# Two pairs of copies left unordered, and one band of input loaded earlier, in a dilated neighborhood attention kernel

## The chip, the cores and the metric

The kernel runs on one core of a Trainium2 chip. Its time is the device time in microseconds of that core, from one launch. The kernel before takes 312.07 us (median of 3 runs, 311.24 to 313.02). Its profile was taken in an execution of 311.96 us, whose span from the first to the last instruction is 310.2 us. All times below that say when something happens count from the start of that span.

## What is computed

Each pixel of a 224 x 224 image with 192 channels attends to a 7 x 7 neighborhood with dilation 2, that is, to every second pixel of a 13 x 13 window, which is moved inward at the border. Cut to what matters:

```python
def reference(x, wqkv, wo):
    B, H, W, C = x.shape              # 1, 224, 224, 192, bf16
    ks, dil = (7, 2)
    qkv = x @ wqkv
    q, k, v = ...                     # three slices of C channels
    r0 = clip(row - half, 0, H - 1 - (ks - 1) * dil)   # the same for columns
    nidx = (rows[:, None, :, None] * W + cols[None, :, None, :])   # 49 neighbors
    kn, vn = take_along_axis(kf, nidx), take_along_axis(vf, nidx)
    logits = einsum('bnc,bnkc->bnk', qf, kn) * C ** -0.5
    p = softmax(logits)
    o = einsum('bnk,bnkc->bnc', p, vn) @ wo
```

Because of the dilation, rows and columns of even and of odd number never meet: the image falls into four images of half the size, and each of them has a plain 7 x 7 neighborhood.

## The kernel before

The weights are folded first: `aw` holds products of the query and key weights, so that a projected query can be multiplied with the raw input; `WP` holds the product of the value and output weights. What follows is a loop over steps. A step is 8 rows of one row parity, and has seven ticks. A tick computes scores (`s_84`, `s_85`, two banks of PSUM in turn), takes the exponential on ScalarE (`p_sb`), multiplies it with the values (`y_86`, `y_87`), divides on VectorE (`o_sb`) and stores from SyncE. Beside it, each step prepares the next: projected queries (`pg` to `ga`, `gb`), values (`pv` to `vw`), raw keys in the layout that the matmul wants (`xa`, `xb`, copied by GpSimd from `xt`), and the edges of the queries at the border of the image (`pe` to `ge`).

The input comes in bands of 16 image rows, transposed by the DMA; a band has three parts and `xt` holds four bands:

```python
    def load_xt(b, parts=((0, 3),)):
        t = XT[:, (b + 3) % 4]
        for (k0, k1) in parts:
            nc.sync.dma_start_transpose(out=t[:, k0:k1]..., in_=xp[16 * (b % NJ): ...])
```

The tiles `xb` carry, beside keys, one-hot rows and columns that add the mask to the scores. For the third and fourth of them they are copied from one of the first two by SyncE, 224 KB in each of two DMAs:

```python
    def spread_onehots(k, q=nc.sync):
        for cc in range(2):
            ps = slice(M0[cc], M0[cc] + 64)
            src = XB[k % 2][ps, 0, cc].rearrange("p n q -> p (n q)")
            if k > 1:
                q.dma_start(out=XB[k][ps, :, cc]..., in_=src.unsqueeze(1).to_broadcast([64, 2, NT * HK]))
```

The values of up to four key blocks go into one PSUM tile of two banks, and two engines take them out. For the first band each takes one bank; for all others each takes one half of the partitions, and the two are declared not to depend on each other:

```python
            for n in range(n0, n1):
                for kt in range(2):
                    for cc in ((k + 1) % 2, k % 2):
                        nc.tensor.matmul(pv[h:h + 64, ...], lhsT=keys(k, rc, cc, kt)[:, n, :], rhs=WP[:, cc, kt, :], ...)   # line 300
            if first:
                for a, eng in enumerate((nc.vector.tensor_copy, nc.scalar.copy)):
                    if n0 + 2 * a < n1:
                        eng(out=VW[...], in_=pv[:, a, :, 0:C]...)                                                         # line 305
                return pv, []
            ins = []
            for cc, eng in ((0, nc.vector.tensor_copy), (1, nc.scalar.copy)):
                ins.append(eng(out=VW[hs, rc, cc, n0:n1, 0:C], in_=pv[hs]...))                                            # line 311
            tc.declare_no_dep(ins[1].ins, ins[0].ins, reason="the two read different quadrants of the banks")
            return pv, ins
```

The edge projections fill one tile of two banks as well, with VectorE on the first and ScalarE on the second (lines 346 and 347). There are eight of them: one for band 0, and one for each two bands after it.

```python
            g = work.tile([128, 3, 2, LB, 3], BF, name="ge", tag=f"ge{nb}", bufs=2)
            nc.vector.tensor_copy(out=g[:, 0:2]..., in_=pt[:, 0, 0:12 * LB])
            nc.scalar.copy(out=g[:, 2]..., in_=pt[:, 1, 0:6 * LB])
```

The tiles `pg`, `pv` and `pe` share two PSUM buffers in turn, so a tile waits until the copies of the last but one are done. Within a step (`si`) the ticks (`ti`) call, among others:

```python
            T = s_stage(rc, j, i, ...)
            ...                                   # values, queries, edges of the next step
            if si == 3 and ti == 1:
                spread_onehots(3)
            ...
            if si == 2 and ti < 3:
                load_xt(3, ((ti, ti + 1),))
            if (rc, j) == (0, NJ - 3):
                if ti < 3:
                    load_xt(NJ, ((ti, ti + 1),))
            elif ti in (0, 2, 4) and (si == 3 or si > 3 and rc == 0):
                load_xt(j + 2 + (rc == 0), ((ti // 2, ti // 2 + 1),))
```

The helper by which the kernel tells its scheduler that two instructions need no order, which the change uses too:

```python
    def apart(ops, reason="they are in different banks or quadrants"):
        tc.declare_no_dep(ops[1].ins, ops[0].ins, reason=reason)
```

Of the kernel before, what the change touches and what calls it, by code (L numbers as in the profile page):

```python
# [31 lines left out]
def kernel(  # L32
# [7 lines left out]
    nc = tc.nc  # L40
    B, H, W, C = x.shape
# [25 lines left out]
    def load_xt(b, parts=((0, 3),)):  # L67
        if not (0 <= b <= NJ):
            return
        t = XT[:, (b + 3) % 4]  # L70
        for (k0, k1) in parts:
            nc.sync.dma_start_transpose(out=t[:, k0:k1].rearrange("p t r c -> p t (r c)"),
                                        in_=xp[16 * (b % NJ): 16 * (b % NJ) + 16, :, 128 * k0:128 * k1].rearrange("r j c -> (r j) c"))
        xt[b] = t
# [17 lines left out]
    VW = const.tile([128, 2, 2, NT, VS], BF, name="vw")  # L92
# [115 lines left out]
    def apart(ops, reason="they are in different banks or quadrants"):  # L208
        tc.declare_no_dep(ops[1].ins, ops[0].ins, reason=reason)
# [21 lines left out]
    for blocks in ((((0, 128, 0), ("e0", 0, "mo0", 64)), ((128, 64, 0), ("e1", 0, "mo1x", 64))),  # L231
                   (((64, 128, 0), ("m2", 64, "xe2", 0)), ((0, 64, 64), ("m1", 64, "xe1", 0)))):
        pt = ps_go.tile([128, 2, 512], F32, name="prA", tag="go")
# [3 lines left out]
        ops = []  # L237
# [45 lines left out]
    def keys(k, rc, cc, kt):  # L283
        return (XA[k % 3] if kt == 0 else XB[k % 4])[:, rc, cc]

    def half(k, cc):
        return 64 * ((k + cc) % 2)

    def v_unit(k, rc, n0, n1):


        first = (k, rc) == (0, 0)

        def emit():
            pv = ps_go.tile([128, 2, 2, 256], F32, name="pv", tag="go")
# [3 lines that stand above are left out]
                        h = half(k, cc)  # L299
                        nc.tensor.matmul(pv[h:h + 64, (n - n0) // 2, (n - n0) % 2, 0:C], lhsT=keys(k, rc, cc, kt)[:, n, :],  # L300
                                         rhs=WP[:, cc, kt, :], start=(kt == 0), stop=(kt == 1))
            if first:
                for a, eng in enumerate((nc.vector.tensor_copy, nc.scalar.copy)):
                    if n0 + 2 * a < n1:
                        eng(out=VW[:, rc, :, n0 + 2 * a:n0 + 2 * a + 2, 0:C],  # L305
                            in_=pv[:, a, :, 0:C].unsqueeze(1).to_broadcast([128, 2, 2, C]))
                return pv, []
            ins = []
            for cc, eng in ((0, nc.vector.tensor_copy), (1, nc.scalar.copy)):
                hs = slice(half(k, cc), half(k, cc) + 64)  # L310
                ins.append(eng(out=VW[hs, rc, cc, n0:n1, 0:C],  # L311
                               in_=pv[hs].rearrange("p a b c -> p (a b) c")[:, 0:n1 - n0, 0:C]))
            tc.declare_no_dep(ins[1].ins, ins[0].ins, reason="the two read different quadrants of the banks")
            return pv, ins
        return emit
# [7 lines left out]
    def edge_item(b):  # L323

        nb = 2 if b else 1
        LB = 16 * nb

        def emit():
            t = XT[:, (b + 3) % 4:(b + 3) % 4 + nb]
            pt = ps_go.tile([128, 2, 512], F32, name="pe", tag="go")  # L330
            pg = pt[:, :, 0:12 * LB].rearrange("p k (g m b r c) -> p k g m b r c", g=2, m=2, b=nb, r=16)
            lo = [t[:, :, k, :, 0:3] for k in range(3)]
            hi = [t[:, :, k, :, S - 3:S] for k in range(3)]
            el = ((("e0", lo[0]), ("e1", lo[1])), (("xe1", lo[1]), ("xe2", lo[2])))
            ml = ((("m0", lo[0]), ("m1", lo[1])), (("me1", lo[1]), ("me2", lo[2])))
            mh = ((("mo0", hi[0]), ("mo1x", hi[1])), (("m1", hi[1]), ("m2", hi[2])))
            oh = ((("xo0", hi[0]), ("xo1", hi[1])), (("o1", hi[1]), ("o2", hi[2])))
            for g, lists in enumerate(((el, el), (ml, mh), (oh, oh))):
                for par in range(2):
                    for i in range(2):  # L340
                        for h in (1, 0):
                            w, r = lists[h][par][i]
                            nc.tensor.matmul(pg[64 * h:64 * h + 64, g // 2, g % 2, par], lhsT=AW[w][:, 64 * h:64 * h + 64], rhs=r,
                                             start=(i == 0), stop=(i == 1))
            g = work.tile([128, 3, 2, LB, 3], BF, name="ge", tag=f"ge{nb}", bufs=2)
            nc.vector.tensor_copy(out=g[:, 0:2].rearrange("p g m l c -> p (g m l c)"), in_=pt[:, 0, 0:12 * LB])
            nc.scalar.copy(out=g[:, 2].rearrange("p m l c -> p (m l c)"), in_=pt[:, 1, 0:6 * LB])
            for k in range(nb):
                ge[b + k] = g[:, :, :, 16 * k:16 * k + 16]
        return emit  # L350
# [243 lines left out]
    for si, (rc, j) in enumerate(steps):  # L594
        v_q, q_q = [], []
        v_old, v_late = v_late, []
        if si + 1 < len(steps):
            rn, jn = steps[si + 1]
            q_q = q_items(rn, jn)
            v_q = v_units(jn, rn)  # L600
            if rn == rc:
                v_q, v_late = [], v_q
        plan = None
        if si == 0:
            vb, vc = v_units(0, 1), v_q
            plan = [[va[2]], [q_q[1]], [va[3], q_q[2]], [q_q[3]], [q_q[0]], [vb[0]], [vc[0]]]
        if si == 1:
            vd = v_q
            plan = [[q_q[1], vb[1]], [q_q[2], vc[1]], [vb[3]], [vb[2]], [q_q[0], q_q[3]], [vc[2]], [vc[3], vd[0]]]
        if si == 2:  # L610
            plan = [[q_q[1]], [q_q[2], vd[1]], [v_q[3]], [v_q[0]], [q_q[0], q_q[3], vd[2]], [v_q[1]], [v_q[2], vd[3]]]
        if plan:
            v_q, q_q = [], []
        for ti, i in enumerate(range(NQ - 1, -1, -1)):
            P = pend[0] if len(pend) > 1 else None
            T = s_stage(rc, j, i, v_close(P) if P else ())
            if P:
                out_stage(P, True)
            spare = None
            if si > 0 and ti == 2 and v_q:  # L620
                spare = v_q.pop()()
            if P and ti == 1 and si > 0:
                opened()
                P = None
            if ti == 0 and si + 2 < len(steps) and si > 0:
                make_keys(*keys_of.get(si, steps[si + 2])[::-1])
            if si > 0 and ti == 4 and q_q:
                q_q.pop(0)()
            for k, unit in enumerate(plan[ti] if plan else ()):
                u = unit()  # L630
                if ti == 2 and k == 0:
                    spare = u
            if v_q and ti in (3, 5, 6):
                v_q.pop(0)()
            if q_q and ti in (0, 1, 4):
                q_q.pop(int(ti < 2))()
            if P:
                opened(spare)
            if v_old and ti < 2:
                v_old.pop(0)()  # L640
            if v_late and ti in (3, 5):
                v_late.pop(0)()
            if si == 0 and ti == 0:
                make_keys(1, 1)
            if si == 1 and ti == 1:
                spread_onehots(2)
            if si == 1 and ti == 3:
                spread_masks(2, 4, 32)
            if si == 3 and ti == 1:
                spread_onehots(3)  # L650
            if si == 1 and ti == 4:
                make_keys(2, 1)
                mask_rows(2, 1, nc.gpsimd.tensor_copy)
            if si == 2 and ti == 0:
                spread_masks(0, 2, 64)
            if (rc, j) == (0, NJ - 3) and ti == 3:
                spread_masks(5, 4, 32)
                mask_rows(5, 3, nc.gpsimd.tensor_copy)
            if si == 2 and ti < 3:
                load_xt(3, ((ti, ti + 1),))  # L660
            if (rc, j) == (0, NJ - 3):
                if ti < 3:
                    load_xt(NJ, ((ti, ti + 1),))
            elif ti in (0, 2, 4) and (si == 3 or si > 3 and rc == 0):
                load_xt(j + 2 + (rc == 0), ((ti // 2, ti // 2 + 1),))
            pend.append(T)
            for _ in range(min(4, len(held))):
                held.pop(0)()
            if si == len(steps) - 1:
                warm(1, ps_go.tile([128, 512], F32, name="idle", tag="go")[:])  # L670
        assert not v_q and not q_q, (si, len(v_q), len(q_q))
# [49 lines left out]
```

## Time and profile before

| what | value |
|---|---|
| time, median of 3 | 312.07 us |
| span of the profiled execution | 310.2 us |
| TensorE busy | 291.3 us, 94% |
| VectorE busy | 258.6 us, 83% |
| ScalarE busy | 249.8 us, 81% |
| GpSimd busy | 244.2 us, 79% |
| mean DMA rate | 141 GB/s |
| granted TensorE clock | 0.999 |

In the profile PE is TensorE, PEld its weight loads, DVE VectorE, ACT ScalarE, POOL GpSimd and SP SyncE; the DMA issues of SyncE are listed as SPq. A group is named by its line in the kernel, its engine, its operation and its tiles, the output ahead of the arrow. Matmuls overlap each other and their ends are modelled, so that a high share of TensorE says that it had work at hand, not that it ran at its peak. The list of waits names the waiter, what ended its wait, the idle time in all, the number of times and the longest. The chain of waits is followed back from the last instruction, at each step to what released it. The timeline lists instructions by start, with their duration, and in brackets the idle time of the engine ahead of them and what ended it.

### The profile page before, as it was taken

The page shows a single profiled execution, that of the slowest core. Times are in us where ns is not written, and L with a number is a line of the kernel's source. Part 1 is how long each engine was busy: PE and PEld are TensorE (multiplying, and loading weights), DVE is VectorE, ACT ScalarE, POOL GpSimd, SP SyncE. Part 2 cuts the span into 40 slices and gives each one's busy share as a digit, 9 for nine tenths or more (in the row PEclk, how much of TensorE's full clock was granted, in tenths as well). Part 3 has the DMA queues.
Part 4 walks back from the last instruction along what each step waited for, and adds up shares of the span by engine and source line. Part 5 has one row for each costly group of instructions (what it writes and reads, how often), then busy time and mean ns, then how long its engine had stood idle before and what let it go on. Part 6 is the DMA issues. An engine that isn't in the chain of part 4 may idle for free.

```text
span 310.2 us, 17615 instructions
## 1 busy us (share of the span) xinstructions
PE 291.3 (94%) x7484; PEld 271.6 (88%) x7485; DVE 258.6 (83%) x602; ACT 249.8 (81%) x409; POOL 244.2 (79%) x511
## 2 busy tenths in 40 slices
PE   7878999998999999999999999999999999999983
PEld 3457989997999999999999999999999999899862
DVE  7756998886888988888888988889888987889874
ACT  2357989896889978899788997889978897899841
POOL 8497989797888868888588795997858898885950
PEclk9999999999999999999999999999999999999999
DMA  7996458899969487395973967929869295321144
GB/s 163 216 164 150 107 136 141 189 215 188 187 149 187 106 187 136 85 161 138 174 160 82 171 154 136 178 78 195 144 132 189 62 197 137 82 69 28 27 125 120
DMA packets 112774, 43.78 MB, mean 141 GB/s; under 512 B 87520, under 2 KB 112266, under 8 KB 112696
## 3 DMA queue, kind: packets, MB, share of 16 engines
q1 hardware_dynamic: 109634, 40.59, 65.4%
q0 software_dynamic: 2400, 1.63, 2.5%
q8 instruction: 58, 0.95, 1.4%
q10 hardware_dynamic: 662, 0.45, 0.6%
q14 instruction: 20, 0.16, 0.2%
HBM read 0.29 MB, written 19.35 MB: 63 GB/s over the span
## 4 chain that ended last, share of the span: by engine, by line
PE 74%; DVE 12%; issue 5%; ACT 5%; DMA 2%; SPq 0%; DVEq 0%
PE pv L300 18%; PE pg L389 18%; PE y_86 L475 10%; PE s_84 L462 8%; PE s_85 L462 8%; PE y_87 L475 7%; DVE o_sb L550 5%; DVE vw L311 3%; DVE rs L549 2%; ACT p_sb L465 2%; DMA xt<-in_x_dram 1%; ACT vw L311 1%; PE y_87 L206 1%; PE prA L236 1%; ACT ga_96 L393 1%
## 5 line engine op out<-in xcount | busy, mean ns | idle before, releaser
L311 DVE CAST vw<-pv 64x768 bf16<-64x768 f32 (+1 forms) x112 | 95.5, 854 | 15.9 <-PE pv L300 13.5
L475 PEld LDWEIGHTS <-p_sb 128*64 128x64 bf16 (+1 forms) x1540 | 98.8, 106 | 9.3 <-issue 7.4
L475 PE MATMUL y_86<-vw,p_sb 128*64 128x193 bf16 (+1 forms) x840 | 85.1, 247 | 4.0 <-DVE o_sb L550 3.9
L389 PE MATMUL pg<-xt,aw 128*64 128x106 bf16 (+3 forms) x1008 | 84.4, 289 | 3.9 <-ACT vw L305 0.9
L311 ACT CAST vw<-pv 64x768 bf16<-64x768 f32 (+1 forms) x112 | 79.8, 712 | 5.2 <-PE pv L300 3.1
L475 PE MATMUL y_87<-vw,p_sb 128*64 128x193 bf16 (+1 forms) x672 | 69.0, 247 | 1.0 <-DVE o_sb L550 0.6
L550 DVE TENSOR_TENSOR o_sb<-y_86,rs 128x384 bf16<-128x384 f32 x104 | 58.0, 557 | 3.6
L389 PEld LDWEIGHTS <-aw 128*64 128x64 bf16 x1008 | 53.7, 110 | 7.5 <-issue 3.5
L465 ACT ACTIVATE p_sb<-s_85 128x448 bf16<-128x448 f32 x98 | 53.7, 548 | 3.4 <-PE s_85 L462 2.6
L465 ACT ACTIVATE p_sb<-s_84 128x448 bf16<-128x448 f32 x98 | 53.7, 548 | 3.0 <-PE s_84 L462 2.1
L462 PEld LDWEIGHTS <-xa_89 128*64 128x64 bf16 x532 | 46.5, 110 | 1.6 <-issue 1.4
L462 PEld LDWEIGHTS <-xa_88 128*64 128x64 bf16 x532 | 46.3, 110 | 0.3
L550 DVE TENSOR_TENSOR o_sb<-y_87,rs 128x384 bf16<-128x384 f32 x78 | 43.5, 557 | 2.7
L462 PEld LDWEIGHTS <-xa_90 128*64 128x64 bf16 x476 | 42.0, 110 | 0.4 <-issue 0.2
L462 PEld LDWEIGHTS <-xb_92 128*64 128x64 bf16 x420 | 35.5, 109 | 0.6 <-issue 0.5
L462 PEld LDWEIGHTS <-xb_91 128*64 128x64 bf16 x420 | 34.9, 109 | 0.0
L393 ACT CAST ga_97<-pg 128x848 bf16<-128x848 f32 x28 | 24.2, 866 | 8.4 <-PE pg L389 8.4
L393 ACT CAST ga_96<-pg 128x848 bf16<-128x848 f32 (+1 forms) x28 | 23.9, 853 | 8.5 <-PE pg L389 7.7
L300 PE MATMUL pv<-WP,xa_88 128*64 128x192 bf16 x280 | 29.3, 247 | 1.3 <-ACT vw L305 0.9
L462 PEld LDWEIGHTS <-xb_93 128*64 128x64 bf16 x364 | 30.4, 110 | 0.0
L300 PE MATMUL pv<-WP,xa_89 128*64 128x192 bf16 x280 | 29.4, 247 | 0.1
L462 PEld LDWEIGHTS <-xb_94 128*64 128x64 bf16 x336 | 27.6, 109 | 0.0
(166 smaller groups left out, 1064.3 us busy)
## 6 DMA issues: line engine op xcount, KB each, us to landing
out_dram<-o_sb SPq DMA_DIRECT2D x155, 96.0 KB
out_dram<-o_sb SPq DMA_DIRECT2D x26, 60.0 KB
xt<-in_x_dram SPq DMA_TRANSPOSE x40
out_dram<-oall SPq DMA_DIRECT2D x6, 96.0 KB
out_dram<-oe POOLq DMA_DIRECT2D x27, 18.0 KB, 3.1
out_dram<-o_sb POOLq DMA_DIRECT2D x25, 18.0 KB, 3.2
xb_93<-xb_91 SPq DMA_DIRECT2D x2, 224.0 KB
xb_94<-xb_92 SPq DMA_DIRECT2D x2, 224.0 KB
```

Source lines behind the costliest of these rows:

```text
L206: nc.tensor.matmul(bank, lhsT=zero[:, 0:128], rhs=zero[:], start=True, stop=True, skip_group_check=True)
L236: nc.tensor.matmul(pt[p0:p0 + cn, k, 0:C], lhsT=w[:, c0:c0 + cn], rhs=w[:, C:2 * C], start=(i == 0), stop=(i == 1))
L300: nc.tensor.matmul(pv[h:h + 64, (n - n0) // 2, (n - n0) % 2, 0:C], lhsT=keys(k, rc, cc, kt)[:, n, :], rhs=WP[:, cc, kt, :], start=(kt == 0 ...
L311: ins.append(eng(out=VW[hs, rc, cc, n0:n1, 0:C], in_=pv[hs].rearrange("p a b c -> p (a b) c")[:, 0:n1 - n0, 0:C]))
L389: nc.tensor.matmul(pr[64 * h:64 * h + 64, g, a_ - 4 * g:b_ - 4 * g, :], lhsT=AW[w][:, 64 * h:64 * h + 64], rhs=xt[b][:, k, l, 3:S - 3], st ...
L393: return eng(out=dst[:, 6:S].rearrange("p s (g r) -> p s g r", r=4)[:, :, g0:g1], in_=pr[ps, g0:g1].rearrange("p g r s -> p s g r"))
L462: nc.tensor.matmul(o[h:h + 64, s0:s1, rs], lhsT=keys(k, rc, cc, kt)[:, n, :], rhs=(A, Bt)[kt][:, cc, CW * n + s0:CW * n + s1, rs], start=( ...
L465: nc.scalar.activation(out=T.p[:].rearrange("p a b -> p (a b)"), in_=ps[:, 0:4 * QW * BR], func=ACTF.Exp)
L475: return nc.tensor.matmul(o, lhsT=T.p[:, pos, 64 * nxt:64 * nxt + w], rhs=VW[:, T.rc, cc, n, 0:C + 1], start=start, stop=True, skip_group_ ...
L549: nc.vector.reciprocal(out=rs[:], in_=y[:, :, C:C + 1])
L550: nc.vector.tensor_tensor(out=o[:, t - t0], in0=y[:, :, 0:C], in1=rs[:].to_broadcast([128, 2, C]), op=ALU.mult)
```

## The change

It has three parts. The two copies of the first values, and the two of each edge projection, read different banks of one PSUM tile; they are now declared independent, so that the second engine need not wait for the first. The first values also hand out the list of their copies, so that a later matmul and two VectorE operations that use the other bank of the tile are not ordered behind them. And of the band that is loaded in step 3 (the band with number 4), the parts are issued in ticks 0, 1 and 2 and not in ticks 0, 2 and 4; the one-hot copies to the fourth `xb` tile, which stood in tick 1, go to tick 5. The aim is that engines which could work side by side do, and that the band is there when its edges are projected.

```diff
             if first:
+                ops = []
                 for a, eng in enumerate((nc.vector.tensor_copy, nc.scalar.copy)):
                     if n0 + 2 * a < n1:
-                        eng(out=VW[:, rc, :, n0 + 2 * a:n0 + 2 * a + 2, 0:C],
-                            in_=pv[:, a, :, 0:C].unsqueeze(1).to_broadcast([128, 2, 2, C]))
-                return pv, []
+                        ops.append(eng(out=VW[:, rc, :, n0 + 2 * a:n0 + 2 * a + 2, 0:C],
+                                       in_=pv[:, a, :, 0:C].unsqueeze(1).to_broadcast([128, 2, 2, C])))
+                if len(ops) > 1:
+                    apart(ops)
+                return pv, ops
...
-            nc.vector.tensor_copy(out=g[:, 0:2].rearrange("p g m l c -> p (g m l c)"), in_=pt[:, 0, 0:12 * LB])
-            nc.scalar.copy(out=g[:, 2].rearrange("p m l c -> p (m l c)"), in_=pt[:, 1, 0:6 * LB])
+            apart([nc.vector.tensor_copy(out=g[:, 0:2].rearrange("p g m l c -> p (g m l c)"), in_=pt[:, 0, 0:12 * LB]),
+                   nc.scalar.copy(out=g[:, 2].rearrange("p m l c -> p (m l c)"), in_=pt[:, 1, 0:6 * LB])])
...
-            if si == 3 and ti == 1:
+            if si == 3 and ti == 5:
                 spread_onehots(3)
...
-            if si == 2 and ti < 3:
-                load_xt(3, ((ti, ti + 1),))
+            if si in (2, 3) and ti < 3:
+                load_xt(si + 1, ((ti, ti + 1),))
...
-            elif ti in (0, 2, 4) and (si == 3 or si > 3 and rc == 0):
+            elif ti in (0, 2, 4) and si > 3 and rc == 0:
                 load_xt(j + 2 + (rc == 0), ((ti // 2, ti // 2 + 1),))
```

## The prediction

> **What bounds the kernel now.** I read the page first, then the waits by length, the chain of waits, the timeline of the first 30 us, and the timeline of the DMA issues on SyncE around the only long hole of TensorE.
>
> ```profile
> PE 291.3 (94%) x7484; PEld 271.6 (88%) x7485; DVE 258.6 (83%) x602; ACT 249.8 (81%) x409; POOL 244.2 (79%) x511
> ```
>
> TensorE is busy 94% of the 310.2 us span, so 18.9 us of it are idle in all; a change in the order of copies can win only where those gaps are, or where the pace is set by the copies. The waits by total name what the diff touches (waiter, what it waited for, us in all, times, longest):
>
> ```profile
> ACT ge L347 <- DVE ge L346: 10.0, 8, 2.6
> ACT vw L305 <- DVE vw L305: 2.7, 2, 1.5
> PE pe L343 <- DMA xt<-in_x_dram: 1.5, 2, 1.2
> PE pv L300 <- ACT vw L305: 0.9, 1, 0.9
> PE pg L389 <- ACT vw L305: 0.9, 1, 0.9
> ```
>
> The largest, 10.0 us, is idle time of ScalarE, not of TensorE. The next question is where these lie on the chain of waits. The first values do (start us, us, what):
>
> ```profile
> 17.57 0.97 DVE vw L305
> 18.57 0.81 ACT vw L305
> 19.42 0.85 PE pv L300 x16
> 20.27 0.01 PE s_84 L462
> 20.28 0.02 issue
> 20.31 0.97 DVE vw L305
> 21.27 0.02 issue
> 21.30 0.80 ACT vw L305
> ```
>
> The reader sees two copies of one tile laid end to end, twice, with TensorE behind them. The timeline of TensorE shows the hole at the edge projections of bands 3 and 4, and the tile xb_94 shows when it is first used by TensorE:
>
> ```profile
> 71.24 0.31 PE L343 MATMUL pe<-xt,aw 128*64 128x96 bf16 x4 [0.34 <-DMA xt<-in_x_dram]
> 72.74 0.72 PE L343 MATMUL pe<-xt,aw 128*64 128x96 bf16 x18 [1.20 <-DMA xt<-in_x_dram]
> ```
>
> ```profile
> L300 PE MATMUL pv<-WP,xb_94 x35: 246/246/246, 68.2 to 82.0; 128*64 128x192 bf16 x35
> ```
>
> And the timeline of SyncE says why the band is late (start, duration of the run, what):
>
> ```profile
> 59.64 1.42 SPq L72 DMA_TRANSPOSE xt<-in_x_dram  x1
> 61.15 1.46 SPq L503 DMA_DIRECT2D out_dram<-o_sb  x2
> 62.66 2.22 SPq L185 DMA_DIRECT2D xb_94<-xb_92  x2
> 64.97 1.70 SPq L72 DMA_TRANSPOSE xt<-in_x_dram  x1
> 66.80 1.26 SPq L503 DMA_DIRECT2D out_dram<-o_sb  x2
> 68.52 2.05 SPq L72 DMA_TRANSPOSE xt<-in_x_dram  x1
> 70.67 1.85 SPq L503 DMA_DIRECT2D out_dram<-o_sb  x3
> ```
>
> Each entry starts where the one before ends: the issue queue is the pace here. The store issued at 70.67 belongs to a tile that VectorE finished at 63.53, so SyncE is some 7 us behind the program. It has been since the transposes of band 3 (47.39 to 55.9).
>
> [...] the pairs can overlap in full; the trace agrees, since the pair at 16.50 (L393, two quadrants, not ordered) runs 1.04 and 0.86 us side by side. [...] the third part of band 4 is issued at 68.52 to 70.57 and its wait ends at 72.70, 4.18 us after the start. [...]
>
> **The change, part by part.** The order of instructions on TensorE, VectorE, ScalarE and GpSimd is the same in both programs; only their waits differ. On SyncE the two one-hot copies to xb_94 move behind parts 2 and 3 of band 4 and three stores.
>
> *First values.* Now ACT's copy starts when its own bank is filled and ACT is free: at about 17.4 (its copy of 16.50 ends at 17.36) and not at 18.57. The tile is then released by the later of the two, DVE's at 18.54, so TensorE's pv of 19.42 can start at about 18.57: **0.85 us**. The second pair: pv shifted to 18.6 to 19.4, DVE 19.46 to 20.4, ACT beside it 19.5 to 20.3, and the pg that stood until 22.15 can start at about 20.45: another **0.85 us**, 1.7 together. ScalarE, whose chain (vw, exp, vw, exp, hs) leads on from 21.30 to 24.45, starts it about 1.8 us sooner.
>
> *What is left of it.* GpSimd works without a break from 16.5 to 26.4, and nothing moves that. Its waits after it do go: 0.73 us before 27.13 (a store that waits for VectorE) and 0.80 us before 29.62 (placing the edges, which waits for ACT ge). From there to 46.8 it has hardly a gap, and its mask copies that end at 46.80 release the spread behind which SyncE starts band 3. So I carry 0.73 + 0.80 + 0.13 (the edge copy at 15.09 can start at 14.96) = **-1.7 us** through the front, for TensorE and for SyncE.
>
> *Edge projections, the other six.* ACT ge stood 1.4 us for DVE ge at 113.78 and 153.38, but TensorE at the same place shows only 0.1 us (pv at 114.15, after ACT ge's end at 114.10). VectorE, which does as much as before, closes the chain there. I take 0.05 to 0.1 us each, **-0.4 us**.
>
> *Band 4.* Parts 2 and 3 are issued at 62.66 and about 64.4; with 4.2 us the last lands near 68.6, ahead of 70.56 where TensorE first wants it. The hole of 0.34 + 1.20 = **-1.54 us** goes. But the copies to xb_94 are delayed by what now stands ahead: T2 and T3 1.70 + 2.05 us, three stores 3 x 0.64, gaps of 0.05: about 5.8 us, so they are issued at about 68.4 and 69.2 and not at 62.66. Packets of 1,792 bytes, which here only this copy has, ran from 64.0 to 66.75 before, the last 3.3 us after the second issue began. With part 3 and three stores ahead of them I put the end at 72.2 to 73, 72.5 in the middle. TensorE reads xb_94 at 68.2, and its weight loads wait for both copies in the new program as in the old. [...] it stands from 68.2 to 72.5: **+4.3 us**. GpSimd's second copy into xb_94 (68.49) waits for the first of the two as well; the 5.6 us of work from there to the end of edge placing then ends near 77, before the scores that need it (76.9 before, now some 2.8 us later).
>
> Sum, with both SyncE and TensorE shifted by the front: -1.7 - 0.4 - 1.54 + 4.3 = **+0.7 us**, 312.07 to 312.7.
>
> **Rivals.** *The one-hot copies come in time.* If SyncE is less behind, because stores or transposes are issued faster in the new order, the stall is not there: -1.7 - 0.4 - 1.5, 308.5 us. For it: the program issues them four ticks ahead of their use (seven ticks take 10.0 us, from the first scores at 86.7 to those at 96.7, so 5.7 us), which would do without the backlog. Against it: SyncE has no gap from 47.4 to 79, and nothing was taken off it. *The front's gain dies before 47 us.* GpSimd or the key copies could hold TensorE: then -0.4 - 1.54 + 4.3, 314.4 us. For it: GpSimd is at 96% from 20 to 25 us and 30 to 35 us. Against: its two waits there end on ScalarE and VectorE, which both come sooner. *GpSimd becomes the bound behind xb_94*, its edge placing later than the scores: about 1 us more, 313.7.
>
> **Range and chances.** The uncertain terms are the landing of the one-hot copies (1 us either way) and the front (1.2 to 2.2 us); half a rival each way gives 310.3 to 315.0. Two per cent are 6.2 us: neither the full gain of the first rival nor the sum of the losses reaches it. Faster 0.04, same 0.92, slower 0.04.
>
> **What would show it.** In the changed profile: ACT vw L305 no longer behind DVE vw, the first exp of the kernel near 20.3 and not 21.99; ACT ge <- DVE ge gone from the waits, with TensorE's time per step unchanged after 80 us; PE pe <- DMA xt gone; in its place a wait of TensorE's weight loads for xb_94 of about 4 us near 66.5 to 70.8, and one of GpSimd of about 2.5 us. Wrong would be: no wait for xb_94 (first rival), or a step by step shift that is back at zero by 47 us (second), or edge steps that got visibly shorter.

## The result, and the profile after

The changed kernel takes **316.88 us** (316.62 to 317.37) against 312.33 us for the kernel before on the same chip: a ratio of **1.0151, interval 1.0117 to 1.0184**, 4.6 us slower. A time is the median of all executions, while a ratio leaves out those over 1.5% above the fastest of their kernel, so that it is not the quotient of the two medians. The prediction of 312.7 us, and its range up to 315.0, were too low.

The head of the page after; its second line is the granted clock of TensorE in 40 slices of the span:

```profile
PE 292.4 (93%) x7484; PEld 272.8 (87%) x7485; DVE 258.4 (82%) x602; ACT 251.5 (80%) x409; POOL 243.6 (77%) x511
...
PEclk9999999996999999999999999999999999999998
```

TensorE's busy time is 1.1 us longer for the same instructions, in a span that grew from 310.2 to 315.3 us, and one slice near 74 us has a granted clock of 0.6. Neither was in the prediction. (The page before has 0.999 for the clock of its execution; over 169 other executions of the kernel before it lies between 0.973 and 1.000, with a mean of 0.990.) The list of waits after (waiter, what it waited for, us in all, times, longest):

```profile
PEld L300 <- DMA xb_94<-xb_92: 5.5, 2, 4.7
PE pv L300 <- DMA xb_94<-xb_92: 5.1, 2, 4.5
...
POOL xb_94 L275 <- DMA xb_94<-xb_92: 4.6, 1, 4.6
...
PE pg L392 <- DMA xt<-in_x_dram: 1.3, 1, 1.3
```

ACT ge, 10.0 us in the list before, no longer waits for DVE ge, and TensorE's wait at the edge projections of band 4 is gone. In their place stand the one-hot copies, as predicted in kind, and a wait of 1.3 us for band 1, which the prediction had not seen. The timeline of SyncE shows why the one-hot copies are late:

```profile
62.50 4.12 SPq L72 DMA_TRANSPOSE xt<-in_x_dram  x2
66.72 2.30 SPq L506 DMA_DIRECT2D out_dram<-o_sb  x3
69.47 1.37 SPq L185 DMA_DIRECT2D xb_94<-xb_92  x2
70.94 1.23 SPq L506 DMA_DIRECT2D out_dram<-o_sb  x2
```

Parts 2 and 3 of band 4 and three stores lie ahead of them, and only 0.45 us behind the last store is free. So they are issued at 69.47 and 70.23, when TensorE has already stood since 68.09; it goes on at 72.61 and, for the second one, at 73.59. The next view shows the same stretch in steps of 2 us. Its columns are the stretch, its length, the busy time (and instructions) of PE, PEld, DVE, ACT and POOL, the granted clock, the DMA share and GB/s:

```profile
66.00:68.00 2.00, 2.00 (x60) 1.78 (x56) 1.53 (x5) 1.68 (x4) 2.00 (x3) 1.00 1.27 257
68.00:70.00 2.00, 0.09 (x3) 0.00 (x0) 0.15 (x1) 1.01 (x2) 0.09 (x1) 1.00 1.25 121
70.00:72.00 2.00, 0.00 (x0) 0.00 (x0) 0.00 (x0) 0.00 (x0) 0.00 (x0) 0.60 0.74 181
72.00:74.00 2.00, 0.78 (x7) 0.54 (x9) 0.00 (x0) 0.00 (x0) 1.26 (x2) 0.50 0.79 224
74.00:76.00 2.00, 2.00 (x36) 2.00 (x34) 1.40 (x5) 0.64 (x2) 1.96 (x3) 0.50 1.17 235
76.00:78.00 2.00, 2.00 (x50) 2.00 (x48) 1.34 (x2) 1.22 (x3) 0.99 (x4) 0.70 0.72 131
78.00:80.00 2.00, 2.00 (x61) 1.94 (x57) 1.25 (x5) 1.46 (x3) 0.76 (x5) 1.00 1.14 227
```

From 70 to 72 all five engines stand. Then TensorE is busy without a break from 74 to 76, but gets through 36 matmuls and not 60: at full busy share and half the clock. The clock falls during the wait (at 70.38) and comes back only at 77.21, so the wait of 5.1 us may cost more than 5.1 us; this is tested below.

The difference is placed by the starts of the exponentials on ScalarE, one for each tick, in both profiles (both start their first projection at 12.41 us):

| stretch | before | after | difference |
|---|---|---|---|
| first exponential, at | 21.99 | 19.99 | -2.00 |
| first of step 1, at | 31.90 | 31.39 | -0.51 |
| first of step 4, at | 65.84 | 65.52 | -0.32 |
| step 4 (first of step 4 to first of step 5) | 11.83 | 17.23 | +5.40 |
| first of step 5 to first of step 27 | 216.72 | 216.90 | +0.18 |

The gain of 2.0 us at the first exponential is real, and three quarters of it are gone by the next step. Everything that the change costs is in step 4.

### The profile page after: what moved, and what is told of

Same layout as the page of the kernel before. It is cut to its first block, busy times and chain, and to the rows that moved or that the text cites. A ratio compares the mean times of both kernels' runs of the same rounds, so it can differ in the third digit from the quotient of the medians.

```text
span 315.3 us, 17625 instructions
## 1 busy us (share of the span) xinstructions
PE 292.4 (93%) x7484; PEld 272.8 (87%) x7485; DVE 258.4 (82%) x602; ACT 251.5 (80%) x409; POOL 243.6 (77%) x511
## 4 chain that ended last, share of the span: by engine, by line
PE 66%; DVE 15%; issue 7%; DMA 6%; SPq 2%; ACT 2%; DVEq 0%
PE pv L300 17%; PE pg L392 16%; PE y_86 L478 10%; PE s_84 L465 8%; PE s_85 L465 8%; DVE o_sb L553 7%; PE y_87 L478 6%; DVE vw L314 5%; DMA xt<-in_x_dram 5%; DVE rs L552 2%; SPq L72 2%; DMA xb_94<-xb_92 1%; PE pe L346 1%; ACT p_sb L468 1%; ACT vw L314 1%
## 5 line engine op out<-in xcount | busy, mean ns | idle before, releaser
L300 PE MATMUL pv<-WP,xa_88 128*64 128x192 bf16 x280 | 30.5, 251 | 0.5 <-ACT ga_96 L396 0.3
L300 PE MATMUL pv<-WP,xa_89 128*64 128x192 bf16 x280 | 29.4, 246 | 0.1
```

## The experiments

The theory: the copies to `xb_94` are late behind the transposes and stores; their wait and the half clock after it make the loss, and the front gives little because band 1 lands late. The rivals: the unordered copies themselves do harm; the loss is the wait alone; the front's gain is lost to GpSimd or to nothing that can be moved. Each ratio is to the kernel before, in runs on the same chip. All diffs are to the changed kernel unless it says otherwise.

### The parts apart

**Copies alone** (the changed kernel with loads and one-hot copies as before):

```diff
-            if si == 3 and ti == 5:
+            if si == 3 and ti == 1:
                 spread_onehots(3)
-            if si in (2, 3) and ti < 3:
-                load_xt(si + 1, ((ti, ti + 1),))
+            if si == 2 and ti < 3:
+                load_xt(3, ((ti, ti + 1),))
-            elif ti in (0, 2, 4) and si > 3 and rc == 0:
+            elif ti in (0, 2, 4) and (si == 3 or si > 3 and rc == 0):
```

> Only the copies unordered; loads and one-hot copies as in the kernel before. Theory A (the loss is all in the delayed one-hot copies and what they do to TensorE): 0.3 us gained in the front, as at step 2 of the changed profile, nothing at the later edges: 312.0 us. Rival B (the unordered copies cost something too, through two engines reading one tile or through the new waits): 313 us or more.

Measured: 314.41 us against 314.59, ratio 0.9964 (0.9935 to 0.9994), which stands on 14 of the 22 executions, since one of them took only 310.12 us. The means of all 22 and of all 43 of the kernel before, 313.92 and 314.31 us, give 0.9988 (about 0.9964 to 1.0012). So the copies do no harm of the size of the loss, and this run does not show that they save anything. In its profile band 4 is late once more: TensorE stands 2.56 us at its edge projections.

**Loads and one-hot copies alone** (the kernel before with the reverse of the diff just shown: loads and one-hot copies as changed, copies ordered):

> Only the loads of band 4 and the one-hot copies moved; copies ordered as before. Theory A: the whole loss of 4.6 us and without the 0.3 us of the front: 317.2 us, with TensorE waiting some 5 us for xb_94. Rival B: 315 us or less.

Measured: 318.71 us, ratio 1.0146 (1.0097 to 1.0196). This part alone makes a loss of the same size. Its profile has waits of 4.91 and 0.62 us for `xb_94`, half clock from 72.5 to 79.3 us, and a step 4 of 18.10 us.

**The changed kernel once more**, unedited, beside later runs:

> The changed kernel once more, beside its variants on one chip. Theory A: 1.015 of the kernel before, with some 5 us of wait for xb_94 and TensorE at half clock for about 7 us after 70 us. Rival (the first result was one chip's): below 1.008.

Measured: 317.56 us, ratio 1.0160 (1.0116 to 1.0204); waits of 4.47 and 0.58 us, half clock from 73.8 to 80.6, step 4 17.42 us. Loss, wait and clock all come again.

### How much the wait costs: the one-hot copies at other ticks

Three programs move only the line of the one-hot copies:

```diff
-            if si == 3 and ti == 5:
+            if si == 3 and ti == 1:     # first program
+            if si == 3 and ti == 3:     # second
+            if si == 1 and ti == 2:     # third
                 spread_onehots(3)
```

> The changed kernel with the one-hot copies back in tick 1 of step 3, band 4 still in ticks 0, 1, 2. Theory A: no wait for xb_94; the copies stand ahead of parts 2 and 3, so that part 3 is issued near 66.6 and lands near 70.8, about when it is wanted: a wait for band 4 of 0 to 0.5 us; ratio 0.995 to 0.997. Rival C (the early band collides): 1.000 or more.

> The changed kernel with the one-hot copies in tick 3, behind one store and not three. Theory A: issued about 2 us sooner than in the changed kernel (69.5), wait for xb_94 about 3 us; whether the clock falls tells how long a wait it bears: 1.004 if it stays, 1.010 if it falls. Rival (the loss is not the wait): 1.015 as the changed kernel.

> The changed kernel with the one-hot copies to xb_94 issued in step 1, where SyncE still has gaps, and band 4 in ticks 0, 1, 2. Theory A: neither a wait for xb_94 nor one for band 4, clock 1.0 throughout: 312.3 - 0.3 - 1.5 = 310.5 us. Rival C (the earlier band collides with other transfers, so that a wait stays whatever the one-hot copies do): 312 us or more.

| one-hot copies in | wait of TensorE for xb_94, us | half clock in step 4, us | step 4, us | ratio |
|---|---|---|---|---|
| step 1, tick 2 | none | none | 10.08 | 0.9963 (0.9940 to 0.9986) |
| step 3, tick 1 | none, but 0.42 + 1.12 for band 4 | none | 11.69 | 0.9982 (0.9954 to 1.0009) |
| step 3, tick 3 | 2.60 + 0.88 | 3.4 | 15.23 | 1.0106 (1.0053 to 1.0159) |
| step 3, tick 5 (as changed, second run) | 4.47 + 0.58 | 6.8 | 17.42 | 1.0160 (1.0116 to 1.0204) |

Within step 3, later copies make a longer wait and a longer step. None of the three places tried there is good: at tick 1 they go ahead of parts 2 and 3 of band 4, and band 4 is late as in the kernel before. SyncE has hardly a gap there (from 50 to 77 us the longest is 0.45 us, in the kernel before and in the changed one), and the order chooses who waits. In step 1 both fit: the one-hot copies to the third and fourth tile are issued from 37.55 to 40.71 us, and step 4 takes 10.08 us, without wait or half clock. So of the 17.23 us of step 4 after the change, 5.13 are the wait, and 17.23 - 10.08 - 5.13 = 2.0 us are left for the half clock and whatever else follows the wait.

### Is the half clock part of the loss?

The same wait, but TensorE kept busy through it with 20 matmuls whose result is not used (in the first profile they run from 69.62 us for 4.49 us):

```diff
+            if si == 4 and ti == 2:
+                warm(20, ps_go.tile([128, 512], F32, name="idle", tag="go")[:])
             if si > 0 and ti == 2 and v_q:
```

> The changed kernel with 20 dummy matmuls of 128x512 into a spare PSUM buffer ahead of the values that wait for xb_94, so that TensorE is busy for about 4.3 us of the wait; results are not touched. Theory A1 (5.1 us of wait less 1.5 us of the old hole, plus about 1.8 us lost because TensorE runs at half clock from 70.4 to 77.2 us): the clock stays at 1.0 and the time falls by 1.5 to 2 us, to about 315.1. Rival A2 (the extra loss after the wait is the engines filling up again, the clock is only a symptom): 316.9 us as in the changed kernel.

> The dummy matmuls in the wait again, on the same chip as the changed kernel. Theory A1 (half clock costs about 1.8 us of the loss): 1.5 to 2 us below the changed kernel, ratio to the kernel before 1.009 to 1.010. Rival A2 (only refilling): as the changed kernel within 0.5 us.

Measured: 316.79 us, ratio 1.0101 (1.0043 to 1.0159), and again, on one chip with the second run of the changed kernel, 316.83 us, ratio 1.0133 (1.0092 to 1.0175) against 1.0160. On that chip the means of six executions each are 318.10 us without the matmuls and 316.88 with them: 1.2 us less, with an interval from about 0 to 2.5. Their mean granted clock is 0.978 without and 0.990 with them, against 0.991 for the kernel before, so the half clock of the wait is in the executions at large and not only in those profiled. The profile is clearer; stretches of the same length in the first of these runs, same columns:

```profile
68.00:70.00 2.00, 2.00 (x45) 1.70 (x40) 1.42 (x5) 1.62 (x3) 0.78 (x1) 1.00 1.15 252
70.00:72.00 2.00, 1.95 (x10) 0.88 (x9) 0.00 (x0) 0.70 (x2) 0.00 (x0) 1.00 0.68 178
72.00:74.00 2.00, 2.00 (x10) 0.78 (x8) 0.00 (x0) 0.00 (x0) 0.00 (x0) 1.00 0.89 223
74.00:76.00 2.00, 1.38 (x35) 1.12 (x36) 0.51 (x1) 0.47 (x1) 1.79 (x2) 1.00 0.74 169
76.00:78.00 2.00, 2.00 (x69) 2.00 (x65) 1.87 (x6) 1.63 (x3) 1.96 (x4) 1.00 1.14 251
```

The other engines still stand from 72 to 74, so the wait is there; the clock stays at 1.00, and the first full stretch after it has 69 matmuls, not 36. The wait is as long as in the changed kernel: from 69.6 to 75.02 TensorE does nothing useful but for the first matmuls of the values, from 74.04 on.

A rival is that the extra loss is only the other engines filling up again. They stand here too, so the time from the matmul that waited for the second one-hot copy to the first exponential of step 5 tells the two apart:

| program | half clock after that matmul, us | to the first exponential of step 5, us |
|---|---|---|
| with the matmuls, both runs | 0 | 7.75 and 7.75 |
| one-hot copies in tick 3 | 3.41 | 8.98 |
| changed kernel | 3.62 | 9.16 |
| changed kernel, second run | 4.34 | 9.49 |
| loads and one-hot copies alone | 4.91 | 9.69 |

The excess over 7.75 us grows with the half clock, by 0.36 to 0.40 us for each us of it. **The half clock costs 1.4 and 1.7 us in the two profiles of the changed kernel**, and the wait nearly all the rest; about 0.6 of the 2.0 us left above is not placed. The timed gain of 1.2 us agrees within its interval.

### What the front is worth

**Copies ordered again**, one-hot copies in step 1: the third program of the table with the old order of copies.

```diff
-                        ops.append(eng(out=VW...
+                        (eng(out=VW...
...
-                if len(ops) > 1:
-                    apart(ops)
-                return pv, ops
+                return pv, []
...
-            apart([nc.vector.tensor_copy(out=g[:, 0:2]...
+            ([nc.vector.tensor_copy(out=g[:, 0:2]...
```

> Loads of band 4 in ticks 0, 1, 2 and one-hot copies in step 1, but the copies ordered as in the kernel before. Theory F (the unordered copies gain little, since in the front the landing of bands 1 and 2 ends the waits): as the same kernel with unordered copies (0.996), 0.3 to 0.5 us slower, 0.997 to 0.998. Rival G (the unordered copies keep their 1.7 us): 1.000 or more.

Measured: 312.09 us, ratio 0.9956 (0.9933 to 0.9979), against 0.9963 with unordered copies, which ran on another chip. No worth of the order of the copies shows here. The timeline of TensorE at the edge projections of step 0 says why; first the unordered program:

```profile
27.70 0.91 PE L346 MATMUL pe<-xt,aw 128*64 128x96 bf16 x24 [1.20 <-DMA xt<-in_x_dram]
```

and the ordered one:

```profile
27.69 0.91 PE L344 MATMUL pe<-xt,aw 128*64 128x96 bf16 x24 [0.46 <-DMA xt<-in_x_dram]
```

Both start when band 2 lands, 0.01 us apart. What the unordered program had gained before, it spends waiting: 1.17 us for band 1 and 1.20 here, against 0.74 and 0.46, and the ordered one has its copies' 0.89 + 0.86 instead.

**Band 1 by three plain transfers** (rows of 3,584 bytes) in place of its transpose, with ordered and with unordered copies. Both have the one-hot copies in step 1. The transpose of this band is left out, so the data that follow from band 1 are others than the reference's, in the same shapes:

```diff
-    load_xt(1)
+    for k in range(3):
+        nc.sync.dma_start(out=XT[:, 0, k]..., in_=xp...[128 * 1792 * k:128 * 1792 * (k + 1)]...)
+    xt[1] = XT[:, 0]
```

> The ordered kernel of this call with band 1 read by three plain DMAs of long rows without the transpose, so that its data are not the reference's [...]. Theory F: no wait of TensorE for a band in the first 40 us; as the kernel of this call without that, 0.3 us faster at most, since the ordered copies bound the front before: first tick of step 1 near 31.5.

> The same with unordered copies. Theory F: without the landings the gain of the unordered copies stays: step 1 begins 1.5 to 2.0 us sooner than in the ordered one, and the time is 1.5 to 2 us less. Rival H (GpSimd or another engine takes the gain back before step 1, whatever the bands do): the two within 0.5 us.

Measured: ordered 311.73 us, ratio 0.9947 (0.9922 to 0.9972); unordered 311.86 us, ratio 0.9953 (0.9923 to 0.9984). In the profiles no wait for band 1 is left. The unordered program stands 1.12 us ahead of one projection for something that the profile does not name, and starts the edge projections of step 0 at 27.71 and not 28.67. But these two starts lie 0.14 us behind the landing of band 2, at 27.57 and 28.53: band 2, still transposed, lands no sooner without the transpose of band 1, and it sets the start. Timed, the two are equal. Band 1 alone is not what takes the gain.

**Kind 0 first**: in step 0, make the projection first that needs only two of the three parts of band 1, and load these two together.

```diff
-    load_xt(1)
+    load_xt(1, ((0, 2), (2, 3)))
...
-            plan = [[va[2]], [q_q[1]], [va[3], q_q[2]], [q_q[3]], [q_q[0]], [vb[0]], [vc[0]]]
+            plan = [[va[2]], [q_q[3]], [va[3], q_q[1]], [q_q[2]], [q_q[0]], [vb[0]], [vc[0]]]
```

It was run twice with unordered copies and one-hot copies in step 1, once with ordered copies, and once as an edit of the kernel before with nothing else changed:

> Unordered copies, one-hot copies in step 1, and for step 1 the projection that needs only the first two parts of band 1 goes first, band 1 being loaded in two DMAs. Theory F: the wait for band 1 at 22 us goes or shrinks by 1 us; 0.5 to 1 us faster than without: 0.993 to 0.995. Rival H: no change, 0.996.

> The same program as with kind 0 first, run again beside the two programs that differ from it in one part each: 0.989 of the time before once more (within 0.005).

> As kind 0 first, but with the pairs of copies ordered again. Theory: the saving of the unordered first copies (1.7 us as predicted, 2.0 us seen at the first exponential) was lost to the landing of band 1; with that wait out of the way it comes out at the end: 0.989 + 0.005 = 0.994 to 0.995 of the time before, 1.2 to 2.0 us above the unordered program in the same call. Rival: the order of the copies is worth nothing in the end even then, GpSimd or the landing of band 2 takes it: 0.989 to 0.990, equal to the unordered program within its interval.

> The kernel before with kind 0 of step 0 first and band 1 loaded as parts 0 and 1, then 2; copies ordered, one-hot copies and band 4 as before. Theory (band 1's landing is on the path in the kernel before too): 0.993 to 0.996. Rival (before, ordered copies hide the landing, so that the new order of kinds gains only with unordered copies): 0.999 to 1.001. Its band 4 hole of 1 to 2.6 us at the edge projections stays in both.

| kind 0 first, with | time, us | ratio |
|---|---|---|
| unordered copies, one-hot copies in step 1 | 310.15 | 0.9893 (0.9849 to 0.9937) |
| the same again | 310.80 | 0.9911 (0.9874 to 0.9948) |
| ordered copies, one-hot copies in step 1 | 311.89 | 0.9922 (0.9897 to 0.9947) |
| the kernel before | 314.33 | 1.0018 (0.9990 to 1.0046) |

The last three share a chip. My theory for the third run, that the copies' saving comes out once band 1 is out of the way, isn't borne out: 0.9922 against 0.9911 is no difference within the intervals, though a saving of up to 1.7 us is not excluded by this pair alone. The order of kinds alone gives the kernel before nothing that shows: in its profile, with ordered copies, no wait for band 1 has to go. With the loads and one-hot copies in their new places it is the best version here, 1% ahead of the kernel before and ahead of the changed one by more.

The profiles show where the saving goes when band 1 no longer takes it. In the first run with unordered copies TensorE stands 1.67 us for the next band at the edge projections and starts them at 26.40; the ordered one starts them at 26.41 without a wait. In the second run with unordered copies there is no such wait, and the front is ahead; then it is GpSimd that stands for band 3, in its timeline:

```profile
59.05 0.93 POOL L275 COPY xa<-xt 128x896 bf16<-128x896 bf16 x1 [2.42 <-DMA xt<-in_x_dram]
```

and TensorE behind it, whose scores need the edges that GpSimd places after these copies:

```profile
64.81 0.23 PE L465 MATMUL s<-ga,xa 128*64 128x112 bf16 x2 [1.41 <-POOL ga L371]
```

The ordered program waits 0.52 us there in place of 2.42, and its scores do not wait. In the first run with unordered copies GpSimd stands 1.76 us there and TensorE 1.60. So three landings in a row, of bands 1, 2 and 3, can each end the front, and which one does differs from run to run. In these profiles what the engines save ahead of them becomes a wait.

## Why the prediction was wrong, step by step

| term | predicted, us | in the profiles, us |
|---|---|---|
| front | -1.7 | -0.3 |
| later edge projections | -0.4 | 0 |
| hole at band 4 | -1.54 | about -1.5 |
| TensorE stands for xb_94 | +4.3 | +5.13 |
| half clock after it | not in the sum | +1.4 |
| not placed | | +0.4 |
| sum | +0.7 | +5.1 |

The half clock and what is not placed make the 1.8 us that the sum needs: 17.23 - (11.83 - 1.54) - 5.13 (against the program with the one-hot copies in step 1 it was 2.0). The profiled spans differ by 5.1 us and the timed medians by 4.6.

**"What is left of it": the step that failed first.** The saving at the copies is right: 2.0 us at the first exponential. The first pair runs side by side, for 0.96 us on VectorE from 17.39 and for 0.79 us on ScalarE from 17.07, where it took 0.96 and 0.80 us one after the other; the second pair starts at 19.30 on both engines. The step then asked only what GpSimd does between 16 and 47 us, and carried 1.7 us to the end. It never asked when the next band lands. In the chain of waits after, that is one piece (start us, us, what):

```profile
7.21 14.81 DMA xt<-in_x_dram
```

It ends at 22.02. In TensorE's timeline after, the projection that started at 22.15 before is split by it:

```profile
20.31 0.47 PE L392 MATMUL pg<-xt,aw 128*64 128x318 bf16 x4
22.06 0.65 PE L392 MATMUL pg<-xt,aw 128*64 128x106 bf16 x8 [1.29 <-DMA xt<-in_x_dram]
```

The first four matmuls come 1.84 us sooner, the other eight only 0.4 us (before they started near 22.15 + 0.28 = 22.43). ScalarE is free sooner too, so 0.8 us of the gain outlive this wait; the next one, at the edge projections of bands 1 and 2, takes 0.5 of them. First before, then after:

```profile
22.15 0.93 PE L389 MATMUL pg<-xt,aw 128*64 128x318 bf16 x12 [0.86 <-ACT vw L305]
26.37 0.93 PE L389 MATMUL pg<-xt,aw 128*64 128x318 bf16 x12 [0.34 <-ACT ga_97 L393]
27.63 0.91 PE L343 MATMUL pe<-xt,aw 128*64 128x96 bf16 x24
```

```profile
25.55 0.93 PE L392 MATMUL pg<-xt,aw 128*64 128x318 bf16 x12 [0.34 <-ACT ga_97 L396]
27.31 0.91 PE L346 MATMUL pe<-xt,aw 128*64 128x96 bf16 x24 [0.31 <-DVE rs L552]
```

The view names VectorE, whose work ended at 27.23, but band 2 had landed only at 27.18. A landing is read here as the last of the 16 updates that the transfer makes to its semaphore in the trace. Band 1 and band 2 are issued alike in these programs, and land so:

| profile | copies | band 1 lands | band 2 lands | edge projections start |
|---|---|---|---|---|
| before | ordered | 20.23 | 26.50 | 27.63 |
| loads alone | ordered | 22.43 | 27.67 | 27.80 |
| one-hot copies in step 1 | ordered | 22.25 | 27.55 | 27.69 |
| one-hot copies in step 1 | unordered | 21.52 | 27.56 | 27.70 |
| changed kernel | unordered | 22.02 | 27.18 | 27.31 |
| changed kernel, second run | unordered | 20.77 | 28.81 | 28.95 |

In all eleven profiles with band 1 in one transposing transfer, band 1 lands between 19.88 and 23.31 and band 2 between 26.50 and 28.81, early or late with either order of copies. The profile before has the earliest landing of band 2, and is the only one of these six in which the edge projections do not start 0.13 or 0.14 us behind it. It had 2.2 us to spare at band 1 and 1.0 at band 2. So even by that profile at most about 1.0 us could be carried past the edge projections, and the later landings of the other executions left 0.3. The second rival had foreseen the end of the gain (dead by 47 us, 314.4 us in all), with the wrong cause: it looked to GpSimd and the key copies.

**Later edge projections.** ACT ge's waits went, as predicted, and TensorE's pace did not change: 216.72 and 216.90 us for the rest. It was idle time of an engine that was not the bound; the 0.05 to 0.1 us that I granted each were a guess.

**Band 4.** Right: TensorE no longer waits for it, also with the one-hot copies in step 1, where no other wait hides it. Its last part landed later than forecast, at 70.12 and not near 68.6.

**The stall.** Right in place, cause and kind, and 0.8 us too short. The copies were issued at 69.47 and 70.23, about 1 us later than my 68.4 and 69.2. Two parts of band 4 take 4.12 us to issue where I had 1.70 + 2.05, the three stores 2.30 where I had 3 x 0.64, and SyncE stands 0.45 us before the copies where I had no gap; each landing comes some 3.1 to 3.4 us after its issue, against the 3.3 us that I took from the profile before, so it is the issue that came late. GpSimd's wait was 4.6 us, not 2.5, but it stands beside TensorE and the third rival's cost does not show.

**The half clock.** This was missing from the sum, and no rival held it. With the front at -0.3, no gain at the edges and the stall at 5.13, the sum is +3.3 us and so 315.4, already just above the range. The half clock's 1.4 us and the 0.4 that are not placed take it to what the spans show.

What stays open is the worth of the unordered copies to within some 0.2%. Three pairs that differ in them alone give 0.9963 and 0.9956 (on two chips), 0.9953 and 0.9947, 0.9911 and 0.9922: differences of +0.0007, +0.0006 and -0.0011, each with an interval of 0.003 to 0.005 either way. Together they leave no room for the 0.0054 that 1.7 us would be, but do not exclude a few tenths of a us.

## What to carry to other kernels

Before you carry a saving on one engine forward, look up for each thing that the engine reads next when it lands: the saving lives only as long as the smallest margin on the way, and one profile shows that margin for one execution only (the landing of band 2 differed by up to 2.3 us between profiles). When an issue queue has no gaps (SyncE's longest is 0.45 us here, from 50 to 77 us), moving a transfer ahead of another does not make time, it chooses which of them is late; look for a place much earlier, as step 1 was here, from where no wait for the one-hot copies was left. And where TensorE sets the pace, price a wait like those of step 4, of 2.60 + 0.88 us and more, at more than its length: the half clock after it cost 1.2 to 1.9 us on top, by the table above.

## What was not expected of the hardware

The granted clock of TensorE falls to 0.5 in or just after waits of a few microseconds. It stayed there for 6.8 us after the waits of 4.47, 4.52 and 4.91 us, and for 3.4 us after some shorter ones (2.24 to 2.56 us) and after the two waits of 2.60 + 0.88 us. In the second profile of the changed kernel this wait was enough:

```profile
28.95 1.01 PE L346 MATMUL pe<-xt,aw 128*64 128x96 bf16 x24 [2.24 <-DMA xt<-in_x_dram]
```

The clock is at 0.5 there from 29.4 to 32.8. Waits of 2.33 us (with matmuls in the stall, 23.1 to 26.5) and 2.56 us (one-hot copies at tick 1, 21.7 to 25.1) did the same; yet the wait of 2.56 us in the program with the copies alone left the clock at 1.00, as did those of 1.6 to 1.7 us (kind 0 first, and one-hot copies in tick 3). So in these profiles waits of 2.2 to 2.6 us went either way, and in the stall of the two profiles of the changed kernel the fall came 2.3 and 2.9 us after the last matmul. What decides it is not shown.

In the first 16 us TensorE is slower too. Twelve projection matmuls of 128x424 take 1.62 us from 12.41 us on in the profile before and in the one after, and 0.93 us at 17.60 and 17.41; in the program with one-hot copies in step 1 they still take 1.52 us at 16.60. The granted clock in the two traces has its first record at 16.16 us before and 15.77 us after, and the views count the time ahead of it as 1.00, so the 0.999 before says nothing of the first 16 us. What the clock was there, and what its cost is, is not shown.
